# Moving stage-1 FFT units, raw weight loads and zero stores to other steps in a fused FFT and two-layer mixture-of-experts kernel

## The chip, the cores and the metric

The kernel runs on one core of a Trainium2 chip. The metric is the device time of one execution in microseconds (us): the median of several timed runs. Beside these there is one execution recorded by the hardware profiler, from which all rows of a trace come. The engines are called as the profile calls them: PE is TensorE (matmuls), PEld its weight loads, DVE is VectorE, ACT is ScalarE, POOL is GpSimd, and SP is SyncE, which here only issues DMAs.

## The reference, cut to what matters

```python
X = np.fft.fft(np.fft.fft(x, axis=1), axis=2).real        # x: 8 x 3072 x 256, float32
x = X.reshape(24576, 256)
h = x @ w_in                                              # 256 x 2048
x = (np.maximum(h, 0) + alpha * np.minimum(h, 0)) @ w_out # 2048 x 256
logits = x @ w_gate                                       # 256 x 8 experts
# each token goes to its best expert; an expert takes the first `capacity` tokens that chose it
h = np.maximum(einsum('ecd,edf->ecf', disp, w1), 0)       # 1024 columns per expert
y = einsum('ecf,efd->ecd', h, w2)
out[token] = gate_weight[token] * y[its expert, its slot] # zero for tokens that found no slot
```

The weights w_in and w_out come as 64-bit floats and are handed to the kernel as pairs of 32-bit words. Rows of `out` that belong to tokens without a slot must be zero, so the kernel stores zeros over the whole output before it scatters results into it.

## The kernel before, in words

**Two parts.** The first part (up to about 1090 us of the trace) does, for one of the eight batch entries after the other, the FFT along the sequence and the first layer up to the logits, and routes the tokens. The second part gathers the tokens of each expert and runs both layers for them. The change touches the first part alone.

**Steps.** The first part is a loop over 8 batches (b) of 32 steps each; I count steps through, so step 32b+s is step s of batch b. The function `fstep` is one step: PE computes two products, q (line L476, six matmuls) and p (L486, six matmuls); ACT copies q to qs (L479); DVE makes qm (L480), mp (L490) and mm (L491) from them. Every fourth step, PE adds the logit matmuls of four steps (L503).

**Units.** Everything else is cut into units that are hung onto steps by `at(list, b, s, function, ...)`, into one of three lists: `pre` (issued before the step), `early` (between q and p) and `late` (after the step). Each engine works through its instructions in the order in which they are issued; nothing overtakes. For the FFT of batch nb, while earlier batches are in their steps, the units are, for each of 12 chunks c:

- `load_x`: SP loads 256 KB of x, five steps before stage 1 (batches 2 and up);
- `fold`, three steps before: POOL adds, subtracts and copies (L222, L223, L224);
- `fsplit`, two steps before: ACT rounds the fold to its high part fh (L231), and POOL computes the rest fl (L232);
- `stage1`: PE multiplies (L244: fh twice, then fl, for two column ranges), ACT copies the sum out (L249), SP stores it to the scratch `zd` in DRAM.

After all 12, `load_zk` reads `zd` back for nine `stage2` units (L297), and `transp` transposes them (L323). All stage-1, stage-2, transpose and routing products share one PSUM tile, `mi`.

**Other work of POOL in these steps.** `split` (L463) computes the low part of the operands of a batch's steps, twice two instructions per batch. Routing sends 24 small scatters per batch, one a step (L613), each behind a one-element copy `gate` from the newest mm (L612), which keeps it in place.

**Weights, in batch 0.** Sixteen pieces of raw weights (eight of w_in, called rawi, and eight of w_out, called rawo) are loaded by `wload` (L346) into two buffers, converted by `conv_a` (ACT L355, DVE L356 and L357), `conv_b` (DVE L364 to L366, the last reader of the raw buffer) and `conv_c` (POOL L372, L373), and then used by `w_cs`, `w_t`, `w_b` and `w_h`. `w_h` stores a split piece to DRAM from SP (L396).

**Zero stores.** SP issues 64 DMAs of 384 KB (L803) that write zeros to `out`.

Of the kernel before, what the change touches and what calls it, by code (L numbers as in the profile page):

```python
# [20 lines left out]
S, D, FF, E, F2 = 3072, 256, 2048, 8, 1024  # L21
# [73 lines left out]
def body(tc, ap, out, NB, cap, dbg=None):  # L95
    nc = tc.nc
    ctx = ExitStack()
    with ctx:
        _body(tc, nc, ctx, ap, out, NB, cap, dbg or {})


def _body(tc, nc, ctx, ap, out, NB, cap, dbg):
# [4 lines left out]
    PE, V, A, G, SY = nc.tensor, nc.vector, nc.scalar, nc.gpsimd, nc.sync  # L107
# [58 lines left out]
    zero = rp.tile([128, 256], F32, name="zero")  # L166
# [467 lines left out]
    def consts(c):  # L634
# [21 lines left out]
        g=15.03,  # L656
# [63 lines left out]
    early = {}  # L720
    late = {}
    pre = {}

    def at(d, b, s, fn, *a):
        while s < 0:
            b, s = b - 1, s + 32
        while s > 31:
            b, s = b + 1, s - 32
        assert b < NB
        if b < 0:  # L730
            b, s = 0, 0
        d.setdefault((b, s), []).append(lambda: fn(*a))

    for i in range(1, 8):
        s = 4 * i
        if i > 1:
            for k, t in (("i", s - 10), ("o", s - 8)) if i > 2 else (("i", 0), ("o", 1)):
                at(late, 0, t, conv_a, k, i)
                at(late, 0, t + (i > 2), conv_b, k, i)
                at(pre, 0, t + 1 + (i > 2), conv_c, k, i)  # L740
                if i + 1 < 8:
                    at(late, 0, t + 1 + (i > 2), wload, k, i + 1)
        at(early, 0, max(s - 5, 0), w_cs, i, mi)
        at(early if i > 1 else late, 0, s - 4, w_t, "i", i, mi)
        at(early, 0, s - 3, w_t, "o", i, mi)
        at(early, 0, s - 2, w_b, i, mi)
        at(late, 0, s - 2, w_h, i)
# [6 lines left out]
    for nb in range(1, NB):  # L754
        g0 = 32 * (nb - 1)
        for c in range(12):
            if nb == 1:
                if c > 1:
                    at(pre, 0, c - 3, load_x, nb, c)
                    at(pre, 0, c - 1, fold, nb, c)  # L760
                at(late, 0, c, stage1, nb, c, mi)
                continue
            if nb == 2:
                g, when = 33 + c, late
            elif nb == 3:
                g, when = (50, 53, 56, 59, 61, 62, 64, 66, 67, 68, 69, 70)[c], early
            else:
                g, when = g0 - 24 + 2 * ((15 * c + 5) // 11), early
            at(pre, 0, g - 5, load_x, nb, c)
            at(pre, 0, g - 3, fold, nb, c)  # L770
            at(late, 0, g - 2, fsplit, nb, c)
            at(when, 0, g, stage1, nb, c, mi)
        for u in range(9):
            if nb == 1:
                g = 14 + 2 * u - max(0, u - 5)
            elif nb == 2:
                g = 47 + 3 * u // 2
            else:
                g = g0 + 10 + 2 * u
            at(pre, 0, max(13, g - 2), load_zk, nb, u)  # L780
            at(late, 0, g, stage2, nb, u, mi)
            if nb > 1 or u > 4:
                at(early, 0, g + 1 + (nb == 1 and u == 8), transp, nb, u, mi)
            else:
                at(late, 0, g + 1, transp, nb, u, mi)
        if nb == 1:
            at(late, 0, 30, split, nb, 0)
        else:
            at(late, 0, g0 + 28, split, nb, 0, None, "B")
            at(late, 0, g0 + 29, split, nb, 0, None, "A")  # L790
    for b in range(NB):
        nb = b + 1
        if b:
            at(late, b, 2, split, b, 1, None, "B")
            at(late, b, 4, split, b, 1, None, "A")
            at(late, b, 5, linear, b, 0)
            at(late, b, 6, linear, b, 1)
        if b == NB - 1:
            at(pre, b, 30, lambda: SY.dma_start(out=recp, in_=rec.rearrange("(p j) w -> p j w", p=128)[:, 0:NJ0]))
        if out is not None:  # L800
            for i in range(8):
                r0 = b * S + 384 * i
                at(pre, b, 4 * i + 2, lambda r0=r0: SY.dma_start(out=out[r0 : r0 + 384].rearrange("(p j) d -> p j d", p=128), in_=zero.unsqueeze(1).to_broadcast([128, 3, 256])))  # L803
        if nb < NB:
            rl, r1 = ((2, 3, 4, 5, 6), 7) if nb == NB - 1 else ((11, 12, 13, 15, 16), 18)
            at(late, nb, rl[0], ltrans, b)
            ru, rs = route_units(b)
            for i in range(4):
                at(late if i == 2 else early, nb, rl[i + 1], ru[i])
            for i in range(24):  # L810
                at(pre, nb, r1 + i, rs[i])
# [310 lines left out]
```

## Time and profile before

| | us |
|---|---|
| timed runs, median of 3 (lowest to highest) | 1964.68 (1962.61 to 1967.32) |
| the profiled execution, its time | 1947.84 |
| its span, first to last instruction | 1946.1 |

Share of the span that each engine is busy: PE 97%, PEld 83%, DVE 60%, POOL 57%, ACT 44%. In the profile's 40 slices of 48.7 us PE shows 9 tenths or more in nearly all; the granted clock shows 8 tenths in the second slice and 9 or more in all others. The 16 DMA engines are 9 and 6 tenths busy in the first two slices and mostly 3 to 5 in those up to batch 6.

How to read it: with PE at 97%, time can be won only where PE waits, where it runs at the lower clock, or by giving it less to do. Idle time of the other engines costs nothing by itself. A timeline row says in brackets how long the engine was idle before the instruction and which instruction ended the wait.

### The profile page before, as it was taken

What the parts mean: (1) busy time and instruction counts of PE and PEld (TensorE: products, weight loads), DVE (VectorE), ACT (ScalarE), POOL (GpSimd) and SP (SyncE); (2) the same over time, 40 slices, a digit from 0 to 9 for tenths busy, and PEclk for the clock granted to TensorE, in tenths of its full rate; (3) what the DMA queues carried; (4) which work ended last, traced back from release to release, by engine and by line L of the source; (5) the groups of instructions that cost most, each with busy time, mean ns of one, the idle gap of its engine ahead of it and who ended that gap; (6) DMA issues with size and microseconds to landing.
All of it is one profiled execution on the core that took longest, in us unless ns stands there. A gap on an engine that the chain in (4) does not pass through costs nothing. (4 is left out here: it accounts for less than half of the span.)

```text
span 1946.1 us, 33806 instructions
## 1 busy us (share of the span) xinstructions
PE 1881.3 (97%) x12965; PEld 1614.2 (83%) x12965; DVE 1174.8 (60%) x1684; ACT 846.9 (44%) x1697; POOL 1100.5 (57%) x1230
## 2 busy tenths in 40 slices
PE   8899999899999999999999899999999999999997
PEld 5676677777777777777767699999999999999997
DVE  4898587877878878888799653333333333333331
ACT  3444344434344444443432254544444444445452
POOL 3874464946847658474365275545555555555452
PEclk9899999999999999999999999999999999999999
DMA  9655345344343433432220301011111110101000
GB/s 289 209 163 150 105 145 158 131 123 138 109 149 113 131 127 113 144 125 81 92 82 1 142 16 60 28 39 38 39 39 39 36 39 16 59 17 60 14 9 17
DMA packets 124210, 174.46 MB, mean 90 GB/s; under 512 B 18012, under 2 KB 78237, under 8 KB 123440
## 3 DMA queue, kind: packets, MB, share of 16 engines
q1 hardware_dynamic: 113008, 157.98, 25.6%
q0 software_dynamic: 10752, 12.23, 2.2%
q8 instruction: 102, 1.67, 0.4%
q10 hardware_dynamic: 288, 2.10, 0.3%
q14 instruction: 60, 0.49, 0.1%
HBM read 94.71 MB, written 78.40 MB: 89 GB/s over the span
## 5 line engine op out<-in xcount | busy, mean ns | idle before, releaser
L964 POOL TENSOR_TENSOR gl<-g,gh 128x384 fp32r<-128x384 f32 x240 | 243.7, 1016 | 323.7 <-ACT gh L963 322.8
L480 DVE SCALAR_TENSOR_TENSOR qm<-er,w,qs 128x780 f32<-128x780 f32 x256 | 320.1, 1250 | 157.4 <-ACT qs L479 156.2
L479 ACT COPY qs<-q 128x780 f32<-128x780 f32 x256 | 207.7, 811 | 362.1 <-PE q L476 191.7
L962 DVE SCALAR_TENSOR_TENSOR g<-ng,om,h 128x384 f32<-128x384 f32 x256 | 157.2, 614 | 313.6 <-ACT ng L961 275.3
L976 PE MATMUL y<-gh,WO 128*128 128x384 f32 x1024 | 262.0, 336 | 0.0
L490 DVE SCALAR_TENSOR_TENSOR mp<-p,qs 128x780 f32<-128x780 f32 x256 | 246.0, 961 | 14.1 <-PE p L486 13.7
L491 DVE TENSOR_TENSOR mm<-p,qm 128x780 f32<-128x780 f32 x256 | 245.1, 957 | 0.0
L613 POOL DMA_INDIRECT rec<-recs,idx x192 | 198.0, 1031 | 48.1 <-issue 43.0
L963 ACT CAST gh<-g 128x384 fp32r<-128x384 f32 x256 | 131.6, 514 | 198.0 <-DVE g L962 198.0
L961 ACT ACTIVATE ng<-h 128x384 f32<-128x384 f32 x256 | 125.8, 492 | 175.6 <-PE h L955 175.5
L976 PEld LDWEIGHTS y<-gh,WO 128*128 128x128 f32 x1024 | 186.8, 188 | 0.0
L503 PE MATMUL lg<-mp,Vn 128*32 128x384 f32 x1024 | 185.1, 493 | 0.2 <-DVE mp L490 0.2
L503 PE MATMUL lg<-mm,Vp 128*32 128x384 f32 x1024 | 184.3, 493 | 0.0
L976 PE MATMUL y<-gl,WO 128*128 128x384 f32 x512 | 172.5, 337 | 0.0
L232 POOL TENSOR_TENSOR fl<-xf,fh 128x512 fp32r<-128x512 f32 x72 | 94.3, 1310 | 134.6 <-ACT fh L231 133.9
L998 DVE SCALAR_TENSOR_TENSOR z<-z,z 128x384 fp32r<-128x384 f32 x128 | 71.4, 558 | 162.3 <-ACT z L997 162.3
L1008 PE MATMUL o<-W,z 128*128 128x256 f32 x1152 | 154.7, 284 | 1.2 <-ACT ot L1011 1.2
L612 POOL COPY gate<-mm 128x1 f32<-128x1 f32 x168 | 76.3, 454 | 128.4 <-DVE mm L491 128.3
L1008 PEld LDWEIGHTS o<-W,z 128*128 128x128 f32 x1152 | 146.8, 189 | 1.6 <-ACT ot L1011 1.6
L995 PE MATMUL z<-yh,W 128*128 128x384 f32 x512 | 130.4, 335 | 0.4
L503 PEld LDWEIGHTS lg<-mp,Vn 128*32 128x32 f32 x1024 | 54.9, 110 | 88.3 <-issue 86.5
L222 POOL TENSOR_TENSOR xf<-x 128x254 f32<-128x254 f32 x84 | 90.6, 1078 | 14.6 <-DMA x<-x 13.4
(352 smaller groups left out, 4539.6 us busy)
## 6 DMA issues: line engine op xcount, KB each, us to landing
x<-x SPq DMA_DIRECT2D x96, 256.0 KB
zd<-zw SPq DMA_DIRECT2D x96, 256.0 KB
out_dram<-zero SPq DMA_DIRECT2D x64, 384.0 KB
zk<-zd SPq DMA_DIRECT2D x120, 192.0 KB
r<-w SPq DMA_DIRECT2D x16, 1024.0 KB
abtab<-tm SPq DMA_DIRECT2D x60, 256.0 KB
er<-erd SPq DMA_DIRECT2D x16, 390.0 KB
rawi<-w_in SPq DMA_DIRECT2D x8, 512.0 KB
```

Source lines behind the costliest of these rows:

```text
L479: A.copy(qs, q[:, :, 0:SB])
L480: V.scalar_tensor_tensor(out=qm, in0=e, scalar=w2[:, f : f + 1], in1=qs, op0=ALU.mult, op1=ALU.add)
L490: V.scalar_tensor_tensor(out=mp, in0=p[:, :, 0:SB], scalar=-1.0, in1=qs, op0=ALU.mult, op1=ALU.min)
L491: V.tensor_tensor(out=mm, in0=p[:, :, 0:SB], in1=qm, op=ALU.max)
L503: PE.matmul(l[32 * gi : 32 * gi + 32, 0:384], lhsT=w, rhs=v, start=start, stop=stop)
L613: d = G.indirect_dma_start(out=rec, out_offset=bass.IndirectOffsetOnAxis(ap=st["idx"][:, i : i + 1], axis=0), in_=recs[:, b].rearrange("p ...
L962: V.scalar_tensor_tensor(out=g, in0=ng, scalar=om[:, f : f + 1], in1=ps, op0=ALU.mult, op1=ALU.add)
L963: A.copy(gh, g)
L964: (V if i == 0 else G).tensor_tensor(out=gl, in0=g, in1=gh.bitcast(F32), op=ALU.subtract)
L976: PE.matmul(d["yp"][m][:, 0:384], lhsT=w[:, f, ms], rhs=x, start=(f == 0 and n == 0), stop=(f == NF - 1 and n == 2))
L995: PE.matmul(ps, lhsT=w[:, kd, ms], rhs=x, start=(n == 0), stop=(n == 5))
L1008: PE.matmul(ps, lhsT=x[:, m, js], rhs=w[:, m, :], start=(m == 0 and n == 0), stop=(m == 7 and n == 2))
```

## The change

Three edits, all in the lists of units. No instruction is added or removed; only positions change.

1. **Raw weight loads** (w_in and w_out pieces 3 to 7). `wload` of the next piece is issued right behind the `conv_b` that last reads its buffer, in the same step, instead of one step later. In SP's order this puts it ahead of the next step's x load and zero store, and ahead of `w_h`'s store.
2. **Stage-1 units.** Batch 3: its twelve units move from steps 50, 53, 56, 59, 61, 62, 64, 66, 67, 68, 69, 70 to steps 46, 47, 50, 53, 56, 59, 61, 63, 65, 67, 69, 71, and their loads, folds and splits with them. Batches 4 to 7: chunk 9 moves from step 0 to step 1 of the batch in which it falls; the other eleven stay. With the first also goes the routing of batch 0, which moves by two steps (its logits' transpose from step 43 to 45, its scatters from steps 50 to 73 to steps 51 to 74).
3. **Zero stores.** Batch 0 issues none; batches 1 to 6 issue ten each, every third step, and batch 7 the last four.

```diff
-                at(pre, 0, t + 1 + (i > 2), conv_c, k, i)
                 if i + 1 < 8:
-                    at(late, 0, t + 1 + (i > 2), wload, k, i + 1)
+                    at(late, 0, t + (i > 2), wload, k, i + 1)
+                at(pre, 0, t + 1 + (i > 2), conv_c, k, i)
...
             elif nb == 3:
-                g, when = (50, 53, 56, 59, 61, 62, 64, 66, 67, 68, 69, 70)[c], early
+                g, when = (46, 47, 50, 53, 56, 59, 61, 63, 65, 67, 69, 71)[c], early
             else:
-                g, when = g0 - 24 + 2 * ((15 * c + 5) // 11), early
+                g, when = g0 + (-24, -22, -18, -16, -14, -10, -8, -4, -2, 1, 4, 6)[c], early
...
-            for i in range(8):
-                r0 = b * S + 384 * i
-                at(pre, b, 4 * i + 2, lambda r0=r0: SY.dma_start(out=out[r0 : r0 + 384].rearrange("(p j) d -> p j d", p=128), in_=zero.unsqueeze(1).to_broadcast([128, 3, 256])))
+            for i in range(10 * b - 10, min(10 * b, 8 * NB)) if b else ():
+                r0 = 384 * i
+                at(pre, b, 3 * (i - 10 * b + 10) + 2, lambda r0=r0: SY.dma_start(out=out[r0 : r0 + 384].rearrange("(p j) d -> p j d", p=128), in_=zero.unsqueeze(1).to_broadcast([128, 3, 256])))
         if nb < NB:
-            rl, r1 = ((2, 3, 4, 5, 6), 7) if nb == NB - 1 else ((11, 12, 13, 15, 16), 18)
+            rl, r1 = ((2, 3, 4, 5, 6), 7) if nb == NB - 1 else ((13, 14, 15, 17, 18), 19) if nb == 1 else ((11, 12, 13, 15, 16), 18)
```

## Rows read from the trace of the kernel before

**Rows 1.** The page: busy time, share of the span and instructions of PE and PEld.

```profile
PE 1881.3 (97%) x12965; PEld 1614.2 (83%) x12965; DVE 1174.8 (60%) x1684; ACT 846.9 (44%) x1697; POOL 1100.5 (57%) x1230
```

**Rows 2.** Waits of PE: who waited for whom, us in total, times, longest.

```profile
PE mi L244 <- POOL fl L232: 16.0, 7, 3.3
```

**Rows 3.** PE's timeline: start, us, instruction, count, [idle before it, ended by].

```profile
278.24 0.55 PE L536 MATMUL mi<-con,ls 128*128 128x128 f32 x3 [0.72 <-ACT zw L249]
...
338.29 0.45 PE L476 MATMUL q<-Bh,w22r 128*128 128x390 f32 x1
...
362.66 0.58 PE L244 MATMUL mi<-fl,fr 128*128 128x258 f32 x1 [2.78 <-POOL fl L232]
...
381.14 0.34 PE L476 MATMUL q<-Bh,w12r 128*128 128x390 f32 x1
...
385.86 0.39 PE L244 MATMUL mi<-fl,fr 128*128 128x258 f32 x1 [3.25 <-POOL fl L232]
...
488.67 0.40 PE L244 MATMUL mi<-fh,fr 128*128 128x258 f32 x2
...
489.38 0.34 PE L486 MATMUL p<-Ah,w20r 128*128 128x390 f32 x1
...
491.54 0.34 PE L486 MATMUL p<-Ah,w20r 128*128 128x390 f32 x1
...
496.36 0.39 PE L244 MATMUL mi<-fl,fr 128*128 128x258 f32 x1 [2.14 <-POOL fl L232]
```

**Rows 4.** Windows: busy us of PE, PEld, DVE, ACT, POOL; granted clock; DMA share, GB/s.

```profile
360.00:366.00 6.00, 3.34 (x12) 3.35 (x13) 3.58 (x5) 1.73 (x3) 5.65 (x8) 0.72 0.02 5
...
539.21:662.90 123.69, 120.90 (x931) 92.56 (x932) 102.71 (x124) 54.16 (x107) 82.69 (x100) 1.00 0.41 127
662.90:788.19 125.29, 122.52 (x931) 94.16 (x932) 102.63 (x124) 54.15 (x107) 81.94 (x100) 0.99 0.40 126
```

**Rows 5.** POOL by line, 339.61 to 385.81 us: count | busy us, mean ns | idle before.

```profile
L232 POOL TENSOR_TENSOR fl<-xf,fh 128x512 fp32r<-128x512 f32 x8 | 10.3, 1289 | 4.8 <-ACT fh L231 4.6
...
L222 POOL TENSOR_TENSOR xf<-x 128x254 f32<-128x254 f32 x8 | 8.7, 1093 | 0.2
L223 POOL TENSOR_TENSOR xf<-x 128x254 f32<-128x254 f32 x8 | 5.9, 734 | 0.0
...
L224 POOL COPY xf<-x 128x4 f32<-128x4 f32 x8 | 2.2, 281 | 0.0
```

**Rows 6.** Timeline around the first 2.14 us wait: POOL's rows.

```profile
487.42 1.50 POOL L222 TENSOR_TENSOR xf<-x 128x254 f32<-128x254 f32 x1
...
497.34 1.00 POOL L613 DMA_INDIRECT rec<-recs,idx  x1 [0.15 <-issue]
```

**Rows 7.** Timeline of the same stretch: one row of DVE.

```profile
484.68 3.65 DVE L480 SCALAR_TENSOR_TENSOR qm<-er,w,qs 128x780 f32<-128x780 f32 x1
```

**Rows 8.** Timeline of batch 0: PE's waits that end on ACT.

```profile
90.53 0.66 PE L404 MATMUL mi<-con,wo 128*128 128x128 f32 x4 [1.32 <-ACT zw L249]
...
135.36 0.45 PE L476 MATMUL q<-Bh,w12r 128*128 128x390 f32 x1 [1.14 <-ACT qs L479]
...
155.12 0.63 PE L404 MATMUL mi<-con,wo 128*128 128x128 f32 x4 [2.23 <-ACT tm L201]
```

**Rows 9.** The same stretch: ACT, DVE and SP around one rawo load.

```profile
153.83 0.67 ACT L355 ACTIVATE mo<-rawo 128x512 f32<-128x512 f32 x1 [4.23 <-DMA rawo<-w_out]
...
138.91 0.69 DVE L366 SCALAR_TENSOR_TENSOR fro<-rawo,so 128x512 f32<-128x512 uint32 x1
...
147.02 0.53 SPq L396 DMA_DIRECT2D wo_d<-wod  x1
147.59 0.61 SPq L346 DMA_DIRECT2D rawo<-w_out  x1
```

**Rows 10.** Waits, 66 to 227 us: ACT's and SP's, us in total, times, longest.

```profile
ACT mo L355 <- DMA rawo<-w_out: 13.3, 5, 4.2
...
SPq L211 <- POOL xf L224: 24.8, 6, 7.5
```

More of the change, by code (lines that the diff above doesn't have):

```diff
@@ L739, in _body @@
                 at(late, 0, t + (i > 2), conv_b, k, i)
+                if i + 1 < 8:
+                    at(late, 0, t + (i > 2), wload, k, i + 1)
                 at(pre, 0, t + 1 + (i > 2), conv_c, k, i)
-                if i + 1 < 8:
-                    at(late, 0, t + 1 + (i > 2), wload, k, i + 1)
         at(early, 0, max(s - 5, 0), w_cs, i, mi)
```

## The prediction

> **What bounds the kernel now.** I read the page first, then PE's waits, then PE's timeline for where these waits lie, and last the timelines of the engines that ended them. PE is busy for 97% of the span [rows 1], so the sum is over PE's waits and its slow stretches alone. The largest wait in the first part is one kind: stage 1 waits for POOL's fl, 16.0 us in seven places [rows 2]. The timeline puts three of them into batch 3's units (2.78 and 3.25 us are the larger ones) and four, of 2.14 us each, on chunk 9 of batches 4 to 7; one of those stands [rows 3]. So batch 3 holds 16.0 - 4 x 2.14 = 7.4 us, and the third wait is 7.4 - 2.78 - 3.25 = 1.4 us. Around the 2.78 us wait the granted clock of a 6 us window is 0.72 [rows 4]: part of it ran at 1.2 instead of 2.4 GHz. Two stretches with the same units, one of them with such a dip, differ by 125.29 - 123.69 = 1.6 us [rows 4]; that is a dip's price. Batch 3 has two dips (behind the 2.78 and the 3.25 us wait), the four chunk-9 waits together one. In batch 0, PE waits 1.32, 1.14 and 2.23 us for ACT [rows 8].
>
> **Batch 3's units.** From the fl of step 57, which starts at 339.61, to the fl that ends the 3.25 us wait in step 69 at 385.81, POOL works without a pause of note: 46.2 us, with eight fl and eight folds [rows 5]. It is a queue that is behind, so its length is what counts. By the new list the same stretch, from the fl of step 57 to that of chunk 10 (again step 69), has six fl and five folds; the scatters (one a step) and the operand splits are the same. A fold is 1.09 + 0.73 + 0.28 = 2.1 us, an fl 1.29 us [rows 5]. The queue shrinks by 3 x 2.1 + 2 x 1.29 = 8.9 us to 37.3 us. It starts 1.3 us after step 58 begins (338.29, [rows 3]), so it ends at 38.6 us after that.
>
> When does PE come for it? Step 69 begins at 381.14, 42.85 us after step 58 [rows 3]. In that lie waits of 2.78 and 1.4, a dip of 1.6, and seven stage-1 units where the new list has five. A unit costs PE 489.38 - 488.67 = 0.71 us [rows 3]. Without them the way is 42.85 - 4.2 - 1.6 - 1.4 = 35.6 us; q and the fh matmuls take 1.3 more, so PE wants chunk 10 at 36.9. The wait left over is 38.6 - 36.9 = 1.7 us, in one piece or spread over chunks 7, 8 and 10. Bounds: if the three folds that go are short ones, whose first add takes as little as the second (0.73 + 0.73 + 0.28), the queue is 1.1 us longer and 2.8 us stay; if POOL waits less for DVE than now, none. I widen the upper end to 5 us, since what is left of the queue may meet DVE more often. Gain in waits: 7.4 - 1.7 = 5.7 us.
>
> Of the two dips I count one as gone, 1.6 us, because waits of under 2 us are left; the ends are none and both. The routing units, which move by two steps, no longer share a step with another user of the PSUM tile mi: a wait of 0.72 us goes [rows 3], and one of the same size behind it, in the routing product; I leave 0.2 us each: 1.0 us. Together 5.7 + 1.6 + 1.0 = 8.3 us, ends 2 and 12.
>
> About the dip: the Trainium skill ("TensorE: Matmul & The Clock Gate", section "What's actually happening") says that the window by which the gate judges activity runs freely and is not reset by the kernel. By that rule it is luck which wait draws a dip. The trace agrees: of four equal waits of 2.14 us one did. By the rule alone I would count no dip as gone for good, and the sum would be 1.6 us smaller.
>
> **Chunk 9 of batches 4 to 7.** It looks like 4 x 2.14 us, but I do not count it so. From 487.42, POOL does six things in the old order: the fold of chunk 9, a scatter, the operand split, a scatter, fl, a scatter, which ends at 498.34 [rows 6]. In the new order the fold goes behind the split and fl behind the last scatter: the same six things, with fl last. With the same durations fl ends at 498.34. PE comes for fl later by one p and one q, 491.54 - 489.38 = 2.16 us [rows 3]: at 494.22 + 2.16 = 496.38 instead of 494.22 (the end of the wait, 496.36, less 2.14). The wait is then 1.96 us instead of 2.14: 0.2 us gained, four times, 0.7 us. What could move it: three of the six met DVE's qm, as the fold's first add: it takes 1.50 us [rows 6] where the second, of the same size, takes 0.73 [rows 5], and qm, at work until 488.33 [rows 7], ends in its midst. Each such meeting costs 0.77 us. With none in the new order fl ends at 496.0, before PE comes; with one more the wait is 2.7 us. So the ends are 8.6 us gained and 2.3 lost. I take 0.7, since in this stretch DVE issues one qm per step in either order.
>
> **Raw weight loads.** In batch 0, ACT waits 13.3 us in five places for rawo [rows 10], and what it evicts for PE stands behind. One of them as it runs: conv_b's last read of the buffer ends at 138.91 + 0.69 = 139.6, but SP issues the load at 147.59, behind w_h's store at 147.02, which waits for POOL; ACT gets it at 153.83, after 4.23 us of waiting [rows 9], and PE waits 2.23 us behind that [rows 8]. Issued at 139.7 with the same 6.2 us to landing, it is there at 146, before ACT's wait begins at 149.6. The same holds for the loads behind the 1.32 and the 1.14 us wait. All three go: 4.7 us. Ends: 1 us, if DVE, busy for most of that stretch, is then what PE waits for; 7 us, if the smaller waits of batch 0 go along. What SP now does behind the waiting load: a zd store, then the next x load. The x loads already stand 4.1 us on average behind POOL's folds (24.8 us in six, [rows 10]), and that is the cover.
>
> **Zero stores.** SP issues as many as before, eight fewer in batch 0 and two more per batch after. The DMA engines are 0.41 busy in such a batch [rows 4] and no PE wait there ends on a DMA: 0, with ends of 1 us on either side.
>
> **Sum.** 8.3 + 0.7 + 4.7 + 0 = 13.7 us. The profiled execution would take 1947.84 - 13.7 = 1934.1 us. The timed median lies 16.8 us above the profiled execution; I carry that over unchanged: 1964.68 - 13.7 = 1951.0 us.
>
> **Rivals.**
>
> *A, POOL gets through faster than its old queue says* (20%). In the new order its instructions meet fewer qm's, so that chunk 9 and batch 3 lose all waits: 1.7 + 1.6 more in batch 3, 4 x 1.96 = 7.8 more at chunk 9, so 11.1 us more: 1939.9 us. For it: the meetings are a third of the wait's making and depend on order. Against it: POOL is as full as before in those steps, and qm comes every step. The Trainium skill ("SBUF — State Buffer", section "Who interferes with whom") has it that the pair of ports is locked by whoever issues first for the whole instruction, so order alone decides; the trace agrees in the add named above.
>
> *B, the waits only move* (14%). In batch 3, chunks 6 and 7 now sit right behind the operand splits of steps 60 and 61, so the change does not do there what it says. If 5 us of waits and both dips stay, batch 3 gives 7.4 - 5 + 1.0 = 3.4 us; chunk 9 loses 2.3; the loads give 2: together 3.1 us, 1961.6 us, the same by what this kernel's measurement can tell (0.2%, 3.9 us).
>
> *C, slower: SP stands at the moved loads* (6%). Each waits for conv_b, and the next x load for batch 1 stands behind it in SP's queue. If DVE's conv_b ends later than POOL frees the x buffer, then fold and stage 1 are late by the difference. Six x loads stand behind such a load. To undo 13.7 us and cost 4 more, each would have to be 3 us late beyond its cover of 4.1 us, so conv_b 7 us later than now; the time would then be 1964.68 - 13.7 + 18 = 1969 us. Against it: DVE reaches conv_b in the step in which it is issued.
>
> **How the numbers follow.** My forecast has 60%. Its own range runs from 1945 (the upper ends of batch 3 and of the loads, 3.7 and 2.3 us less) to 1957 (the lower end of batch 3, 6.3 us more). The range for 8 in 10 takes in A and B to just beyond their times, 1938 to 1962; it leaves out C and about a third of A and of B. Faster by over 0.2% means under 1960.8: all of my forecast and A and a quarter of B, 84%; the rest of B is the same, 10%; C is slower, 6%.
>
> **What would show it.** Right: stage 1's wait for fl falls from 16.0 us to about 9.5, with about 2 us at each of four chunk 9's, now in step 1, and under 3 us in batch 3; ACT no longer waits for rawo, and the three PE waits of batch 0 are gone; SP's raw loads stand directly behind conv_b. Wrong: no wait at chunk 9 (then A); waits of 4 us or more at chunks 7 to 10 of batch 3 (B); PE waiting in batch 0 for POOL's xf of batch 1, with SP held at L346 (C). A new PE wait on a DMA in batches 1 to 7 would upset the zero stores' nought.

## The result, and the profile after

The changed kernel takes 1938.93 us (median of 4 runs, 1938.00 to 1942.17) against 1963.64 us before (4 runs, 1960.56 to 1967.32). The ratio is 0.9876, 95% interval 0.9858 to 0.9894: 20.8 to 27.9 us less, where 13.7 were forecast. The same kernel, run again on two other occasions, gave 0.9897 (0.9875 to 0.9919) and 0.9906 (0.9890 to 0.9923), 20.2 and 19.8 us by the medians. The three intervals share 20.8 to 21.6 us, so I go by about 21 us. The direction and the places were right; the sum was too small.

The profiled execution after takes 1938.96 us, with a span of 1937.2 us, only 8.9 us shorter than the profiled one of before. Two executions are not two kernels; the section on why the prediction was right says what that cost it. First the line of the page after that answers to [rows 1] (busy time, share of the span and instructions of each engine):

```profile
PE 1879.1 (97%) x12965; PEld 1612.8 (83%) x12965; DVE 1183.1 (61%) x1684; ACT 846.3 (44%) x1697; POOL 1100.6 (57%) x1230
```

PE is busy for the same 97%, so again its waits and slow stretches are what counts. PE's waits after (who waited for whom, us in total, times, longest):

```profile
PE mi L244 <- POOL fl L232: 8.1, 7, 2.3
PE mi L244 <- POOL xf L224: 5.3, 3, 3.4
...
PE q L476 <- ACT qs L479: 4.4, 3, 2.9
```

The wait for fl has halved, from 16.0 us [rows 2] to 8.1, in seven places as before. PE's timeline (start, us, instruction, [idle before it, ended by]) tells where they lie:

```profile
93.58 1.13 PE L244 MATMUL mi<-xf,f 128*128 128x258 f32 x4 [0.72 <-POOL xf L224]
...
114.96 1.13 PE L244 MATMUL mi<-xf,f 128*128 128x258 f32 x4 [1.14 <-POOL xf L224]
...
335.38 0.45 PE L476 MATMUL q<-Bh,w22r 128*128 128x390 f32 x1
...
354.81 0.39 PE L244 MATMUL mi<-fl,fr 128*128 128x258 f32 x1 [1.14 <-POOL fl L232]
...
361.00 0.39 PE L244 MATMUL mi<-fl,fr 128*128 128x258 f32 x1 [0.77 <-POOL fl L232]
...
373.28 0.45 PE L476 MATMUL q<-Bh,w12r 128*128 128x390 f32 x1
...
377.16 0.39 PE L244 MATMUL mi<-fl,fr 128*128 128x258 f32 x1 [2.30 <-POOL fl L232]
...
487.29 0.39 PE L244 MATMUL mi<-fl,fr 128*128 128x258 f32 x1 [0.96 <-POOL fl L232]
```

- **Batch 3** (354 to 378 us): 1.14 + 0.77 + 2.30 = 4.2 us in place of 7.4, at chunks 7, 8 and 10, which are the ones the prediction named.
- **Chunk 9** (487.29, and 610.17, 733.05 and 856.97 with the same 0.96): 0.96 us where [rows 3] had 2.14.
- **Batch 0**: the waits of [rows 8] are gone, and two waits for POOL's xf are new, 0.72 and 1.14 us.

The half-clock stretches at these places are gone too. Windows of the kernel after (busy us of PE, PEld, DVE, ACT, POOL; granted clock; DMA share, GB/s), of which the first answers to the first of [rows 4]:

```profile
360.00:366.00 6.00, 5.23 (x47) 2.99 (x47) 6.00 (x7) 1.40 (x2) 5.51 (x8) 1.00 0.46 141
372.00:378.00 6.00, 3.70 (x22) 3.29 (x22) 5.94 (x7) 2.43 (x4) 5.79 (x6) 1.00 0.44 137
```

The clock is 1.00 even in the window that holds the 2.30 us wait. Counted from the start of the span, the trace of after is 14.3 us ahead of that of before at step 232: 2.4 at step 32, 10.4 at step 96, and the rest comes in four pieces of 0.8 to 1.4 us, each at a chunk 9. (After began its first step 1.5 us later, 53.15 against 51.63, so the steps themselves gained 15.9.) That is near the 13.7 us forecast, but partly by luck: the trace of before had few half-clock stretches, as the experiments show. In batch 7 after then gives back 5.5 us, by something that no step of the prediction has:

```profile
1011.48 0.81 ACT L479 COPY qs<-q 128x780 f32<-128x780 f32 x1 [7.82 <-remote]
...
1012.34 0.69 PE L476 MATMUL q<-Bh,w22r 128*128 128x390 f32 x1 [2.90 <-ACT qs L479]
```

```profile
1010.00:1015.00 5.00, 2.66 (x8) 2.67 (x9) 2.68 (x3) 1.07 (x2) 0.48 (x1) 0.64 0.02 3
1015.00:1020.00 5.00, 5.00 (x20) 4.79 (x20) 3.61 (x5) 1.35 (x2) 2.51 (x4) 0.68 0.01 0
```

ACT starts one copy some 3 us late, the trace names no engine that it waited for ("remote"), PE waits 2.90 us, and PE runs at the lower of its levels, 1.2 GHz, for about 7 of these 10 us (the windows below the rows lose 0.36 x 5 + 0.32 x 5 = 3.4 us). So the span hides part of the gain. The experiments come back to this gap.

### The profile page after: what moved, and what is told of

The parts are those of the page before. It is cut to its first block, busy times and chain, and to the rows that moved or that the text cites. A ratio compares the mean times of both kernels' runs of the same rounds, so it can differ in the third digit from the quotient of the medians.

```text
span 1937.2 us, 33789 instructions
## 1 busy us (share of the span) xinstructions
PE 1879.1 (97%) x12965; PEld 1612.8 (83%) x12965; DVE 1183.1 (61%) x1684; ACT 846.3 (44%) x1697; POOL 1100.6 (57%) x1230
## 5 line engine op out<-in xcount | busy, mean ns | idle before, releaser
L480 DVE SCALAR_TENSOR_TENSOR qm<-er,w,qs 128x780 f32<-128x780 f32 x256 | 328.0, 1281 | 146.5 <-ACT qs L479 136.7
L476 PE MATMUL q<-Bh,w22r 128*128 128x390 f32 x256 | 97.8, 382 | 2.9 <-ACT qs L479 2.9
```

Source lines behind the costliest of these rows:

```text
L480: V.scalar_tensor_tensor(out=qm, in0=e, scalar=w2[:, f : f + 1], in1=qs, op0=ALU.mult, op1=ALU.add)
```

## Experiments

**How they are read.** Each execution has a span and a mean granted clock c. I split the span into (1 - c) x span, the time lost to the low clock, and c x span, the rest, and give means over all executions of a kernel. On the occasion of the whole change's first rerun the kernel before has 26.9 and 1924.6 us (23 executions). The split is rough. Among executions of this one kernel, 1 us more of counted loss goes with only 0.55 us more of span (the 30 executions below) or 0.71 (these 23), so a counted loss is more than what it costs, and some of a fall in the loss turns up as a smaller fall of the rest. Where it matters I go by the starts of the steps in the traces.

### The kernel before against itself

> The kernel before, unchanged, against itself, for a second trace. The changed kernel came out 24.7 us faster by the timed medians (1963.64 to 1938.93), but only 8.9 us by the two traces (spans 1946.1 and 1937.2), and 14.3 us up to step 232. Theory 1: the trace of before was a lucky execution; an ordinary one carries some 15 us more in a few places (waits for nothing local, or stretches at the lower clock) that this trace lacks. Then the new trace has a span near 1960 us and shows where. Theory 2: executions under the profiler are shorter than others by a fixed amount; then the new trace has 1946 us again while the timed runs stay near 1963.

Measured: 1957.71 us (12 runs) against 1954.13 (30 runs), ratio 1.0017 (1.0002 to 1.0032). The interval leaves out 1 although the kernels are equal, so a timed difference of 0.2%, 4 us, shows nothing by itself. The rest is equal, 1924.5 and 1924.4; the clock loss is 30.8 and 27.8. The 30 runs spread from 1945.8 to 1959.6 us, at clocks of 0.981 to 0.991. So the difference of two clock losses is known to about 3 us from a dozen runs, that of two rests to about 2. The profiled execution here takes 1955.56 us, within the spread of the others, so theory 2, that the profiler shortens executions, is out. Its span, 1953.8 us, is 7.7 us longer than that of the first trace, about half of what theory 1 put there. The trace on which the prediction rests, clock 0.989 and 0.011 x 1946.1 = 21 us lost, was a lucky execution. The four chunk 9's in this second trace of the same kernel (windows, columns as above):

```profile
500.00:506.00 6.00, 5.60 (x26) 5.32 (x30) 3.29 (x4) 1.40 (x2) 5.15 (x9) 0.72 0.54 155
624.00:630.00 6.00, 4.36 (x17) 4.36 (x18) 4.27 (x4) 0.78 (x3) 5.65 (x8) 0.73 0.29 78
749.00:755.00 6.00, 4.17 (x26) 3.78 (x30) 4.82 (x6) 1.77 (x3) 5.64 (x8) 1.00 0.27 69
873.00:879.00 6.00, 4.49 (x19) 4.49 (x20) 4.14 (x4) 1.04 (x3) 5.64 (x8) 0.74 0.31 99
```

Each comes with a wait for fl of 2.11 to 2.13 us. Three of the four drew a half-clock stretch, not one; a window at 0.72 loses 0.28 x 6.00 = 1.7 us. What that costs shows in the starts of steps 94 and 103, around the first of the four, and of steps 158 and 167, around the third, which drew none (PE's timeline of this trace):

```profile
491.55 0.45 PE L476 MATMUL q<-Bh,w22r 128*128 128x390 f32 x1
...
526.91 0.45 PE L476 MATMUL q<-Bh,w12r 128*128 128x390 f32 x1
...
741.99 0.45 PE L476 MATMUL q<-Bh,w22r 128*128 128x390 f32 x1
...
775.82 0.45 PE L476 MATMUL q<-Bh,w12r 128*128 128x390 f32 x1
```

The same nine steps take 35.4 us with the stretch and 33.8 without: a dip costs 1.5 us.

### Each edit alone

```diff
# raw weight loads alone
-                    at(late, 0, t + 1 + (i > 2), wload, k, i + 1)
+                    at(late, 0, t + (i > 2), wload, k, i + 1)
# batch 3 alone (with the routing of batch 0)
-                g, when = (50, 53, 56, 59, 61, 62, 64, 66, 67, 68, 69, 70)[c], early
+                g, when = (46, 47, 50, 53, 56, 59, 61, 63, 65, 67, 69, 71)[c], early
...
# chunk 9 alone
-                g, when = g0 - 24 + 2 * ((15 * c + 5) // 11), early
+                g, when = g0 + (-24, -22, -18, -16, -14, -10, -8, -4, -2, 1, 4, 6)[c], early
# zero stores alone
-            for i in range(8):
+            for i in range(10 * b - 10, min(10 * b, 8 * NB)) if b else ():
...
```

Raw weight loads. 

> Only the raw loads are moved. My term: 4.7 us (three waits of PE for ACT, 1.32 + 1.14 + 2.23 us, go; ACT no longer waits 13.3 us for rawo). The traces of before and after agree with about 3.9 us up to step 32 for this edit and the zero stores together. Rival: the raw loads are fast only because the zero stores are gone from batch 0; then this edit alone gives under 2 us.

Batch 3. 

> Only batch 3's stage-1 units and the routing of batch 0 are moved. My term: 8.3 us (5.7 of waits, 1.6 for a dip of the clock, 1.0 of routing). The traces of before and after give 8.5 us between steps 48 and 72, 6.7 of them in the steps 64 to 72. If the two dips are what makes most of the timed difference, more than 10 us; if the rival that the waits only move is right, under 4 us.

Chunk 9. 

> Only chunk 9 of batches 4 to 7 moves by one step. My term: 0.7 us, since POOL's queue of six instructions ends as before; rival A: 8.6 us, if POOL meets no qm. In the trace of the changed kernel the wait is 0.96 us in each of the four places, 1.2 us less than before, so 4 x 0.8 to 1.2 = 3.2 to 4.8 us, and possibly 1.6 us more for a dip. Waits here: 0.96 us four times.

Zero stores. 

> Only the zero stores are moved. My term: 0, within 1 us. If the raw loads' gain needs the DMA time that the zero stores free in batch 0: this edit gains 1 to 3 us by itself, and the rawo waits of ACT (13.3 us) shrink here too.

| alone | median, before | ratio (95%) | us less by the ratio (95%) | forecast | the rest | clock loss |
|---|---|---|---|---|---|---|
| raw loads | 1950.41, 1954.13 | 0.9980 (0.9969 to 0.9992) | 3.9 (1.6 to 6.1) | 4.7 | -2.2 | -1.8 |
| batch 3 | 1943.26, 1954.13 | 0.9953 (0.9934 to 0.9972) | 9.2 (5.5 to 12.9) | 8.3 | -5.0 | -3.0 |
| chunk 9 | 1946.61, 1954.13 | 0.9969 (0.9955 to 0.9982) | 6.1 (3.5 to 8.8) | 0.7 | -3.0 | -4.1 |
| zero stores | 1953.43, 1953.57 | 0.9997 (0.9980 to 1.0013) | 0.6 (-2.5 to 3.9) | 0 | -1.3 | +2.1 |

The rests add up to 11.5 us, near the whole change's 11.7 (below). **Raw loads**: 0.2% is no more than equal kernels differed by, so the traces carry this one. From the start of step 0 to that of step 32, the eight traces of this document with the new loads take 177.4 to 178.2 us, the six with the old ones 178.5 to 184.8: by the means 4.5 us less. PE's three waits in batch 0, 4.7 us, are gone, and two waits for xf are new, 1.9 us. The trace of this kernel has them without the other edits, and with the zero stores alone ACT still waits for rawo. Lines of waits, first of the raw loads alone, then of the zero stores alone:

```profile
PE mi L244 <- POOL xf L224: 5.2, 3, 3.4
```

```profile
ACT mo L355 <- DMA rawo<-w_out: 9.9, 4, 4.6
```

(3.4 of the 5.2 us is a wait that the kernel before has too, at the start.) With the raw loads alone ACT has no wait for rawo; with the zero stores alone it has 9.9 us, next to 10.6 to 13.3 in the other traces with the old loads. So it is the earlier issue, not the absence of zero stores, that speeds the raw loads. **Batch 3**: fl waits of 12.3 us in all, 16.0 before. Here the wait at chunk 10, 1.92 us, drew a half-clock stretch (a window of this kernel):

```profile
390.00:396.00 6.00, 5.17 (x34) 3.02 (x38) 3.46 (x4) 1.20 (x2) 5.82 (x8) 0.72 0.32 110
```

**Chunk 9**: fl waits of 11.3 us in all, so 4.7 less, and no half-clock stretch at any of its four places. Its 6.1 us (7.5 by the medians) are about nine times the 0.7 forecast. The nine steps around each place take 33.0 us here. At the old place they take 33.8 to 33.9 without a dip and 35.3 to 35.4 with one (20 places in five traces, 9 with a dip). So a shorter wait is worth 0.85 us a place and the dips 9/20 x 1.5 = 0.7: together 4 x 1.5 = 6 us, a little under half of it the clock's.

### The whole change again

> The whole change once more, on the chip of the single edits. There, execution times of the kernel before spread from 1945.8 to 1959.6 us, and its mean granted clock over 30 executions is 0.9858, where its first trace had 0.989: that trace was a lucky execution. Counting (1 - granted clock) x span as time lost by the clock, the kernel before loses 27.8 us and has 1924.4 us besides. By my sum (12.1 us of waits, 1.6 us of clock): 1912.3 besides and 26.2 lost. By the theory that every wait of about 2 us also draws a dip about every second time: the loss falls by 6 to 9 us, to about 20, and the change gains 18 to 21 us here.

Measured: 1933.39 us (6 runs) against 1953.57 (23 runs). The rest falls from 1924.6 to 1912.9, by 11.7 us; the clock loss from 26.9 to 19.3, by 7.6. The forecast had 12.1 and 1.6; the theory that goes by how often waits of 2 us draw a dip, 18 to 21 us in all and a loss of about 20, came out. In this trace ACT's gap in batch 7 is not there, and the span is 1929.4 us, 16.7 below that of before.

> The changed kernel beside it, on the same chip, to have more executions: against the kernel before 18 to 21 us less, of it 6 to 9 us of time lost by the clock and 11 to 13 us of waits.

Measured on another occasion: 1940.43 us (5 runs) against 1960.18 (9 runs). The rest falls by 7.9 us, the clock loss by 11.2. The gap is there again (7.8 us of ACT's idleness). Here the 2.29 us wait at chunk 10 did draw a half-clock stretch (window of this kernel):

```profile
374.00:380.00 6.00, 3.71 (x18) 3.02 (x20) 3.58 (x5) 2.01 (x3) 5.82 (x7) 0.72 0.16 58
```

### The waits kept, PE kept busy in them

The kernel before, with 18 matmuls more in each chunk 9 of batches 4 to 7, put where PE would wait for fl. They write into the bank of p, whose tile is taken ahead of the units for it; their product is used by nothing.

```diff
...
+                if b > 3 and c == 9 and (m, n) == (0, 2):
+                    for _ in range(18):
+                        PE.matmul(pcur[0][:, 0, 0:256], lhsT=rk[:, 4], rhs=rk[:, 0:2], start=True, stop=True)
```

> The kernel before, with 18 matmuls of no use put into the wait of chunk 9 of batches 4 to 7, just ahead of the fl product (into the bank of p, which p overwrites); they take about as long as the wait of 2.14 us. Nothing waits less. Theory that the idle array draws the dips: the loss by the clock falls by 2 to 5 us (four waits, a dip of 1.7 us behind every second one or more) and the time with it. Rival, that the dips come from the kinds of matmul around and not from the wait: no change in the loss. If the fillers outlast the wait: up to 1 us more besides.

Measured: 1952.94 us (12 runs) against 1953.57, ratio 0.9997 (0.9981 to 1.0013). The clock loss falls by 3.8 us to 23.1, the rest grows by 3.0. The matmuls in the first chunk 9, and windows of all four:

```profile
501.80 2.14 PE L247 MATMUL p<-rk 128*128 128x256 bf16 x18
```

```profile
500.00:506.00 6.00, 5.87 (x41) 5.16 (x41) 4.93 (x6) 1.73 (x3) 5.66 (x6) 1.00 0.15 44
624.00:630.00 6.00, 5.84 (x42) 5.27 (x41) 4.93 (x6) 1.41 (x3) 5.63 (x7) 1.00 0.05 15
748.00:754.00 6.00, 5.86 (x41) 5.35 (x41) 4.94 (x5) 1.40 (x2) 5.49 (x8) 1.00 0.09 29
872.00:878.00 6.00, 5.84 (x42) 5.33 (x41) 4.93 (x6) 1.40 (x2) 5.49 (x7) 1.00 0.11 40
```

The product of fl comes no earlier than before, yet the clock stays at 1.00 in all four, and the nine steps around each place take 33.8 to 33.9 us, as they do with an empty wait and no dip. So at this place it is PE's idleness that draws the low clock, not the kinds of matmul around it. The evidence is four places of one execution. That the loss falls by 3.8 us agrees, but is near the 3 us by which equal kernels differ. The time did not fall as the theory wants, by 2 to 5 us: its interval, 3.7 us less to 2.5 more, holds the 2.7 us that four places at 9/20 x 1.5 would give, and nothing as well. Why the rest grows by 3.0 I can't read from the rows: 2.14 us of matmuls stand for waits of 2.11 to 2.14 us.

Counted over the traces of this document: chunk 9 at its old place, with nothing put into the wait, drew 9 half-clock stretches in 20 places (5 traces); with a wait of about 0.95 us none in 28 (7 traces); filled, none in 4. The places are not independent draws: three of the five traces have one stretch, always at the third place, and the other two have three, at the other places. Each of the five has at least one; the filled one has none.

### Batch 3's units spread further

```diff
-                g, when = (46, 47, 50, 53, 56, 59, 61, 63, 65, 67, 69, 71)[c], early
+                g, when = (46, 47, 50, 52, 53, 56, 58, 59, 62, 65, 67, 70)[c], late if c in (3, 6) else early
```

With this list, and chunk 9 one more step later (2 for 1 in its list):

> The whole change, and further: batch 3's units at steps 46, 47, 50, 52, 53, 56, 58, 59, 62, 65, 67, 70 (those of 52 and 58 after p), and chunk 9 of batches 4 to 7 two steps on instead of one. By the account of POOL's queue, every fl is ready before PE wants it: at chunk 8, 12.3 us after the start of step 58 for 16.2; at chunk 10, 28.4 for 31.3. The 8.1 us of waits for fl in the trace of the changed kernel go, so 8 us less than the changed kernel, and no dip is left in batches 3 to 7 but by chance. If POOL's queue only moves to the chunks that now come earlier, no gain, with waits at chunks 3 to 6.

With this list alone:

> The changed kernel with batch 3's units at steps 46, 47, 50, 52, 53, 56, 58, 59, 62, 65, 67, 70, and chunk 9 as in the change. In the traces of the run with both further moves, steps 64 to 72 took 3.3 us less than in the changed kernel, and the steps around chunk 9 nothing less: its wait of 0.96 us turned into two waits of 0.4 and 0.6 us for DVE's mm. So here 3.3 us less than the changed kernel, with four waits of 0.96 us left, and the same time as the run with both moves within 1 us. If the second move helped after all, 3 us more than that run.

Measured: 1931.32 us (6 runs) with both, 2.1 us below the whole change on the same occasion, where 8 were expected; 1935.18 us (4 runs, 1933.15 to 1939.03) with the list alone, 5.2 below the whole change (1940.43) beside it, where 3.3 were expected, and 0.9875 (0.9860 to 0.9891) of before. These are few runs; in the traces, steps 32 to 76 take 170.8 to 171.7 us with the further list (three traces) and 173.8 to 175.9 with the list of the change (five): 3.4 us less by the means. PE's waits, first with both, then with the list alone:

```profile
PE p L486 <- DVE mm L491: 5.1, 11, 0.7
PE mi L244 <- POOL xf L224: 5.1, 3, 3.2
```

```profile
PE mi L244 <- POOL fl L232: 3.8, 4, 1.0
...
PE p L486 <- DVE mm L491: 1.4, 4, 0.4
```

The list takes the last waits for fl out of batch 3 (what is left is 4 x 0.95 at chunk 9). Moving chunk 9 on takes those out too, and PE then waits for DVE instead, 5.1 us against 1.4: from step 76 to 232 it takes 592.5 us, as the others do (592.0 to 593.2), so it gains nothing.

### ACT's gap in batch 7

The whole change, then the version with the list above, both with the zero stores as in the kernel before.

```diff
-            for i in range(10 * b - 10, min(10 * b, 8 * NB)) if b else ():
+            for i in range(8):
...
```

> The whole change but its zero stores, which stand as before: eight in every batch. In three of the five traces with the whole change or a spread of it, ACT starts one copy qs (L479) of batch 7 some 3 us late, after 7.8 to 7.9 us of idleness whose end the trace puts down to no engine; PE then waits 2.9 us, and in the first of them the step starts fall back by 5.5 us with the low clock behind it. In none of the seven traces of the other kernels is there such a gap. Theory 1 (the late copy comes with the zero stores, of which the last is issued in step 11 of batch 7): the gap is not there in this trace, and the median lies 1 to 5 us below the whole change, some 23 us below the kernel before. Theory 2 (it comes with the other edits, or by chance, and the zero stores are worth nothing): the median is within 2 us of the whole change, some 20 us below before; a gap in this trace would rule theory 1 out, its absence alone would not decide.

> The whole change with batch 3's units spread further, and the zero stores as before. Theory 1 (zero stores): no gap of ACT in batch 7, median 1 to 5 us below the same kernel with the changed zero stores, so 26 to 30 us below the kernel before. Theory 2: some 24.5 us below before, as with the changed zero stores (25.0 there). Either way no wait of stage 1 for fl in batch 3, four of 0.95 us at chunk 9, and no half-clock stretch at these places.

Measured: 1940.66 us (6 runs) and 1936.34 us (5 runs) against 1964.16 (11 runs), ratios 0.9881 (0.9858 to 0.9904) and 0.9856 (0.9831 to 0.9881). Both traces have the gap; the first one's row:

```profile
1012.01 0.81 ACT L479 COPY qs<-q 128x780 f32<-128x780 f32 x1 [8.02 <-remote]
```

So the changed zero stores don't cause it. The medians, 23.5 and 27.8 us below before, are those that theory 1 named, but on this occasion the kernel before was slower than on the others, and the whole change did not run beside it; what the zero stores are worth is better read from the run with them alone. The gap stands in five of the seven traces with both lists changed (not in the two from one occasion) and in none of the seven others. Steps 232 to 255 take 70.2 to 70.4 us without it, 73.5 in these two traces, where no half-clock stretch comes with it, and 74.6 to 75.8 in the three where one does. What it is stays open.

## Why the prediction was right, and where not

**What held.** The bound, the seven places, and the sizes of three of the four terms. From the starts of the steps in the traces: batch 3 (steps 32 to 76) takes 174.8 us with the new list and 183.3 with the old (means of five and six traces), 8.5 us less where 8.3 were forecast; batch 0 (steps 0 to 32) 4.5 less where 4.7 were; the zero stores gave nothing, as forecast. Chunk 9 (steps 76 to 232) takes 592.6 us and 598.2 (seven and five traces), 5.6 less where 0.7 were. Most of what was missing from the sum is there. Inside the terms errors of both signs cancelled:

- *Batch 3's waits*, "the wait left over is 38.6 - 36.9 = 1.7 us": 4.2 measured. PE's half of this sum was right: from step 58 (335.38) to step 69 (373.28) are 37.9 us, less waits of 2.15 (one of 0.24 for ACT among them) 35.75; 35.6 was forecast. POOL's half was not. Its stretch from the fl of step 57 (336.70) to the end of chunk 10's (377.11) is 40.4 us, not 37.3. Its rows by line after (count | busy, mean ns | idle before), to be held against [rows 5], and two of the timeline:

```profile
L222 POOL TENSOR_TENSOR xf<-x 128x254 f32<-128x254 f32 x6 | 8.2, 1360 | 0.0
L232 POOL TENSOR_TENSOR fl<-xf,fh 128x512 fp32r<-128x512 f32 x6 | 7.7, 1282 | 6.2 <-ACT fh L231 6.2
L223 POOL TENSOR_TENSOR xf<-x 128x254 f32<-128x254 f32 x5 | 3.7, 732 | 0.0
```

```profile
367.44 1.28 POOL L232 TENSOR_TENSOR fl<-xf,fh 128x512 fp32r<-128x512 f32 x1 [1.59 <-ACT fh L231]
368.67 1.47 POOL L222 TENSOR_TENSOR xf<-x 128x254 f32<-128x254 f32 x1
```

  The count was right (six fl, five folds; the sixth add is the next chunk's). But the first add takes 1.36 us on average where it took 1.09: five of the six take about 1.5, not half of them, which I read as more meetings with DVE's qm, and 5 x 0.27 = 1.4 us go there. And POOL had caught up at one place, where it stood 1.59 us for ACT's fh (the other 4.6 of the 6.2 us lie ahead of the stretch, as they did before): a queue that empties is no longer a sum of its parts. Together 3.0 of the 3.1 us by which the stretch is longer than forecast; the small rows (copies, scatters) moved both ways. The 4.2 us are within the "upper end" that I had left open, 5 us. So the waits gave 3.2 us where 5.7 were forecast, and the dips made up for it.
- *The dips in batch 3*: one counted as gone, both gone in this trace. Over the traces, the two long waits of the old list (2.78 to 2.80 and 3.23 to 3.32 us) drew a stretch in 11 of 12 places (six traces), four of these twice as long; the longest wait of the new list, 1.9 to 2.3 us at chunk 10, drew one in 2 of 5. That is 4.3 us of counted loss per execution before and 0.7 after.
- *Chunk 9*, "the same six things, with fl last": the wait is 0.96 us where 1.96 was forecast. The order was as worked out, the meetings were not. POOL and DVE around it, after:

```profile
479.15 1.87 POOL L463 TENSOR_TENSOR Al<-Af,Ah 128x780 fp32r<-128x780 f32 x1
479.61 2.26 DVE L480 SCALAR_TENSOR_TENSOR qm<-er,w,qs 128x780 f32<-128x780 f32 x1
480.99 1.47 POOL L222 TENSOR_TENSOR xf<-x 128x254 f32<-128x254 f32 x1
...
483.24 0.18 POOL L612 COPY gate<-mm 128x1 f32<-128x1 f32 x1
483.55 1.02 DVE L480 SCALAR_TENSOR_TENSOR qm<-er,w,qs 128x780 f32<-128x780 f32 x1
...
484.59 0.19 POOL L612 COPY gate<-mm 128x1 f32<-128x1 f32 x1
...
485.94 1.30 POOL L232 TENSOR_TENSOR fl<-xf,fh 128x512 fp32r<-128x512 f32 x1
```

  The split and the fold stand back to back and share one qm, which takes 2.26 us where the next takes 1.02; both one-element copies run free, at 0.18 and 0.19 us. "DVE issues one qm per step in either order" was true and beside the point: as I read these rows, what counts is how many of POOL's instructions are due while one runs. The prediction drew here on the Trainium skill ("SBUF — State Buffer", section "Who interferes with whom"), by which whoever issues first holds the shared ports for its whole instruction; the trace agrees, and it is the number of such meetings that I had wrong.
- *Raw loads*. SP issues the load of [rows 9] right behind conv_b's last read, which now ends at 137.41 + 0.69 = 138.1, and ACT converts it without a wait. From the timeline after, DVE, SP's queue and ACT:

```profile
137.41 0.69 DVE L366 SCALAR_TENSOR_TENSOR fro<-rawo,so 128x512 f32<-128x512 uint32 x1
...
138.18 0.40 SPq L346 DMA_DIRECT2D rawo<-w_out  x1
...
149.34 0.69 ACT L355 ACTIVATE mo<-rawo 128x512 f32<-128x512 f32 x1
```

  Of the 4.7 us forecast the three waits went, "all three", and 1.9 us came back, so 2.8 by these waits; the steps gained 4.5. What is late next is POOL: the folds that end the waits at 93.58 and 114.96 stand behind its conv_c and follow it without a pause; PE, no longer held by ACT, now comes before them. The prediction asked what SP does behind the waiting loads and not what POOL does. SP does stand at them, for conv_b, 13.8 us in five, and no fold is late for it.
- *Zero stores*: nothing, as forecast.

**What failed: chunk 9's term, and the clock in it.** The prediction gave chunk 9 of batches 4 to 7 0.7 us, for a wait that falls from 2.14 to 1.96 us, and counted nothing for its dips. The wait fell to 0.96, which is worth 0.85 us a place, and the dips went: none in 28 places where 9 of 20 had one, 0.7 us a place. That makes 6 us, with 5.6 by the steps and 6.1 (3.5 to 8.8) by the runs of that edit alone. The clock's whole term is "of the two dips I count one as gone, 1.6 us". Counted are 7.6 and 11.2 us (19.3 us lost instead of 26.9, 20.6 instead of 31.8), too much by what the split overstates. Of these, chunk 9's places give 9/5 x 1.7 = 3.1 and batch 3's 4.3 - 0.7 = 3.6. Two things were wrong with the term. I read the price of waits from one execution in which they were cheap: one dip in four at chunk 9, where five traces have 9 in 20. And I took from the rule that the window runs freely ("TensorE: Matmul & The Clock Gate", section "What's actually happening", in the Trainium skill) that it is luck which wait draws a dip, and so counted little as gone. The traces agree with the luck as far as equal kernels have the dips in other places. But the chances hang on the wait: those of 2.1 us drew a stretch in 9 of 20 places, those of 0.96 us in none of 28. Halving a wait was worth more than half.

**The baseline.** "The timed median lies 16.8 us above the profiled execution; I carry that over unchanged." It was no overhead to carry over: after, the profiled execution (1938.96) lies on the median (1938.93), and equal kernels spread by 14 us on one occasion, their times following the clock. On other occasions the median of the kernel before lay between 1953.6 and 1964.2 us. Much of the 16.8 us was luck of one execution, and its missing dips were part of the gain.

**The rivals.** A gave 1939.9 us, next to what was measured, and it is not what happened: it had chunk 9 and batch 3 without waits, and they keep 0.96 and 4.2 us. Its mechanism, fewer meetings with qm, did its work at chunk 9 and the opposite in batch 3. B is refuted by the shorter waits at chunk 9, by ACT's waits for rawo, which went, and by the time. But one of its signs came: 4.2 us of waits at chunks 7 to 10 of batch 3, where "4 us or more" stood for B and "under 3" for the forecast. The signs "about 2 us" at chunk 9 and "about 9.5" in all failed the other way (0.96 and 8.1). C's signs came too (SP stands at the loads, PE waits for xf), but its consequence didn't.

## What to carry to other kernels

Judge a wait on PE by its own length and by what it does to the clock behind it: here waits of 2.1 us cost 1.5 us more in 9 of 20 places, waits of about 0.95 us in none of 28, so shortening them pays before they are gone. Take the clock's part of a forecast from several executions, since one trace may show one stretch in four where the next shows three. And when two engines get into each other's way, look at which instructions are due at the same time, instead of counting instructions: at chunk 9 the same six cost POOL less in another order, in batch 3 fewer of them cost more each.

## What the runs showed of the hardware that I had not expected

The mean granted clock of one and the same kernel went from 0.981 to 0.991 over 30 executions on one occasion, and the times follow it (correlation -0.82) over a spread of 14 us. What is left once the clock is taken out agreed between two sets of that occasion (1924.5 and 1924.4 us), but on two others it was 1927.1 and 1930.1 for the same kernel, so kernels are to be compared within an occasion. A stretch of PE work of 2.14 us with results that nobody uses, put into a wait, left the clock at 1.00 behind it in four places of four. Of these versions those with batch 3 spread further have the lowest ratios, 0.9875, 0.9876 and, with the old zero stores, 0.9856, but the last one's interval (0.9831 to 0.9881) holds the other two; only the steps of batch 3 show that the further list is the faster one.
